# Weight conversion moved into the attention, parked in DRAM, and a re-ordered first round: one core, float32 arithmetic from float64 weights

## The chip, the cores and the metric

The kernel runs on one core of a Trainium2 chip. Its engines work side by side, each on its own list of instructions, in order: PE (TensorE, with PEld for its weight loads), DVE (VectorE), ACT (ScalarE), POOL (GpSimd) and SP (SyncE), which here only issues DMAs. The metric is the device time of one execution in microseconds. Times of parts come from the profile of one execution.

## The reference

Two layers follow each other. Linear attention with a decay per head gives x; a mixer works on x first along the tokens and then along the channels, each time with two matrices, a relu between them, and a residual.

```python
# q, k, v: (4 batches, 8 heads, 768 tokens, 64), float32; lam: one decay per head
for b in range(nb):                          # blocks of 64 tokens
    intra = einsum('bhic,bhjc->bhij', qb, kb) * Dmask       # lam ** (i - j), i >= j
    out[:, :, sl] = einsum('bhij,bhjd->bhid', intra, vb) + einsum('bhid,bhde->bhie', qb * lam_pow, kv_state)
    kv_state = lam_block * kv_state + einsum('bhsd,bhse->bhde', kb * rev_pow, vb)
x = out.transpose(0, 2, 1, 3).reshape(4, 768, 512)
h = maximum(x.transpose(0, 2, 1) @ w_tok1, 0) @ w_tok2      # 768 -> 256 -> 768
u = x + h.transpose(0, 2, 1)
result = u + maximum(u @ w_ch1, 0) @ w_ch2                  # 512 -> 1536 -> 512
```

The weights of the mixer are drawn as float64. The kernel gets them as pairs of 32-bit words and has to make float32 out of them itself.

## The kernel before, in words

**Numbers.** A matrix product in float32 is made of three fast ones: each operand x is split into a rounded high part (ACT copies it into the type float32r) and the rest (DVE or POOL subtracts the high part), and high times high, low times high and high times low are added up in PSUM. Names that end in h and l (c1h, c1l, o6h, o6l, hh, hl) are such pairs.

**Conversion.** `narrow` makes float32 from the two words of a float64 with one ACT pass (Abs of the upper word) and five DVE steps (L348 the sign bit, L351 joins the lower word's top bits to it, L354 limits, L357 shifts, L360 joins). Its steps are put into a list, `waiting`. `later(n)` takes n of them off the list and issues them (n + 1 while more than seven wait); the calls to `later` are written by hand between the parts of the main work. So the order on every engine is the order in which the program issues, and an instruction that waits holds up all that come behind it on its engine.

**Attention.** 16 iterations, each for a pair of heads of one batch (plus two ahead of the first). An iteration holds the scores of the next pair, the outputs of this one, the state, the transposes, and from the fourth on `groups` of the token mixer: `token_hidden` (18 matmuls of 256 columns) and `token_out` (6 of 384 per half), 48 groups in all, of which ten are left over for the first quad. The token weights and the first of six groups of channel weights are converted meanwhile, the latter in four pieces of 512 elements per partition (512 in float64, 1024 words).

**Channel mixer.** The activations lie in SBUF as U, transposed, in six blocks of 512 tokens. Two blocks are worked on together, with a scheme of seven products in place of eight (Strassen's kind): `product(n, s)` multiplies one of seven weight combinations (c1) with one of seven operands o1 to o7, sums and differences of U's blocks. The order of the operands is `PROD = (1, 2, 6, 7, 5, 3, 4)`. A quad n is one pair of blocks (round r = n // 6) against one of six weight groups (g = n % 6); 18 quads in three rounds. Each product is six matmuls of 512 columns into a PSUM bank (a, b or d); bank b is added to several times, and `snap` copies it to SBUF in between (L736) before PE goes on. `whole` adds a bank and a snapshot into an SBUF tile (L740), `relu` makes hh (ACT, L696) and hl of it: by DVE from the SBUF tile (L702), or in the first round, quads 0 to 4, by a second ACT pass and a POOL subtraction (L698, L699). `mm2(n, x, t)` is the second layer, six matmuls, and DVE adds its bank to U (L774). In quad n the products of n alternate with the eight `mm2` of quad n - 1.

**Weights in the first round.** Quad n converts the group of n + 1, four pieces of 512 from `raw_of`, `convert`, with `combine` for the seven sums of the first matrix: POOL forms four sums in a tile `sm` (L509 to L514), ACT and POOL split them into c1h and c1l (L493, L489), and all of this stands in the one list `waiting`. The split weights are kept in DRAM (`keep_c1`, `keep_c2`), and rounds 1 and 2 fetch them from there (`fetch_c1`, `fetch_c2`).

**Operands.** `build(r)` gives the steps that make o1 to o7 of a round: sums by DVE (L660), their split by ACT (L538) and by POOL or DVE (L539). In quad 0 the steps of an operand are issued right before its product; for later rounds they follow the product of the last quad of the round that used the same operand, all of o6's sums there.

Of the kernel before, what the change touches and what calls it, by code (L numbers as in the profile page):

```python
# [9 lines left out]
F32 = mybir.dt.float32  # L10
# [11 lines left out]
def kernel(  # L22
# [28 lines left out]
    P = 128  # L51
# [24 lines left out]
    ident = upool.tile([P, P], F32, name="ident")  # L76
    wa = ctx.enter_context(tc.tile_pool(name="wa", bufs=1))
# [258 lines left out]
    def narrow(raw, a, sg):  # L336
# [11 lines left out]
            lambda: nc.vector.tensor_scalar(  # L348
                out=sg, in0=high, scalar1=0x80000000, scalar2=None, op0=ALU.bitwise_and
            ),  # L350
# [7 lines left out]
                out=a, in0=a, scalar1=3, scalar2=0x40000000, op0=ALU.logical_shift_left, op1=ALU.bitwise_xor  # L358
            ),
            lambda: nc.vector.scalar_tensor_tensor(  # L360
                out=a, in0=a, scalar=0x7FFFFFFF, in1=sg, op0=ALU.bitwise_and, op1=ALU.bitwise_or
            ),
        ]
# [102 lines left out]
    def load_piece(g, i, raw):  # L466
        if i < 2:
            src = c1u[2 * i * P : 2 * (i + 1) * P, g * FG * 2 : (g + 1) * FG * 2]
            nc.sync.dma_start(out=raw.rearrange("p (t f) -> p t f", t=2), in_=src.rearrange("(t p) f -> p t f", p=P))
        else:  # L470
            r0 = g * FG + (i - 2) * P
            nc.sync.dma_start(out=raw, in_=c2u[r0 : r0 + P, :])

    def convert_piece(raw, a, sg):
        return narrow(raw.rearrange("p (n two) -> p n two", two=2), a, sg)
# [3 lines left out]
    def combine(n, pool, a0, a1, s, eng):  # L479

        a0, a1 = (x.bitcast(F32).rearrange("p (t w j) -> p t w j", t=2, w=2) for x in (a0, a1))
        s1, s2, s3, s4 = (s[:, w] for w in range(4))

        def low(sl, src, perm):
            hi, lo = c1s[n]
            lo, hi = lo[:, sl], hi[:, sl].bitcast(F32)
            if perm:
                lo, hi = lo.rearrange("p w t j -> p t w j"), hi.rearrange("p w t j -> p t w j")
            nc.gpsimd.tensor_sub(out=lo, in0=src, in1=hi)  # L489

        def high(sl, src, perm):
            hi = c1s[n][0][:, sl]
            nc.scalar.copy(out=hi.rearrange("p w t j -> p t w j") if perm else hi, in_=src)  # L493

        def raw0():
            c1_tiles(n, pool())
            high(0, a0[:, :, 0], False)
            low(0, a0[:, :, 0], False)
# [454 lines left out]
```

## Time and profile before

| what | us |
|---|---|
| median of three runs (lowest, highest) | 662.24 (661.59, 669.48) |
| the profiled execution | 663.17 |
| its span, first to last instruction | 661.40 |
| attention, to the first product of quad 0 | 192.49 |
| quad 0, with the last ten token groups | 47.76 |
| quads 1 to 5 | 150.30 |
| quads 6 to 17 (to the last product's end) | 249.49 |
| tail | 21.36 |

A busy time is that of an engine's own instructions, overlaps counted once; matmuls overlap, so the mean duration of one (some 0.4 us for 512 columns) is longer than the distance to the next. A row of the groups names line, engine, operation, output and inputs, the shape and the count, then total busy time and the mean of one in ns, then the idle time ahead of them on their engine and what ended it. In a wait row the first name waited for the second.

### The profile page before, as it was taken

Reading aid. Unit: us, or ns where it says so; the run is one execution under the profiler, and the core shown is the slowest. Engines: PE = TensorE matmul, PEld = TensorE weight load, DVE = VectorE, ACT = ScalarE, POOL = GpSimd, SP = SyncE. Lnnn points to the kernel's source line nnn. Section 1 sums busy time; section 2 is a strip of 40 time slices with the busy share of each in tenths; the row PEclk is TensorE's granted clock in tenths of the full one; section 3 lists DMA queues with packets and bytes.
Section 4 is the critical chain, followed back from the end, with each engine's and each line's share of the span. In section 5 each row is a group of like instructions: output and inputs, shape, how many; then the busy total and the mean of one; then the engine's idle time right before and its main releaser. Section 6 shows DMA issues by size and latency. Waiting matters only on the chain. (4 is left out here: it accounts for less than half of the span.)

```text
span 661.4 us, 9534 instructions
## 1 busy us (share of the span) xinstructions
PE 584.0 (88%) x3746; PEld 486.3 (74%) x3746; DVE 416.1 (63%) x649; ACT 201.4 (30%) x376; POOL 220.9 (33%) x198
## 2 busy tenths in 40 slices
PE   6978999799995668697976699999998999999996
PEld 5867988789984546485754578888886888888885
DVE  4578777574526549686696977444556874444554
ACT  2444323233323234234334332121214422121211
POOL 6667734666502363645536530000004300000000
PEclk9989999799998769897979889999999999999999
DMA  9996983747012107164464545644412557244105
GB/s 187 240 235 109 173 154 76 131 91 188 2 33 64 33 3 281 55 264 158 145 257 180 215 176 95 207 175 175 173 71 106 197 99 273 86 175 175 63 1 127
DMA packets 152684, 93.42 MB, mean 141 GB/s; under 512 B 136256, under 2 KB 137792, under 8 KB 152640
## 3 DMA queue, kind: packets, MB, share of 16 engines
q1 hardware_dynamic: 151440, 92.03, 48.9%
q10 hardware_dynamic: 1200, 0.79, 0.4%
q8 instruction: 29, 0.48, 0.3%
q14 instruction: 15, 0.12, 0.1%
HBM read 69.21 MB, written 23.59 MB: 140 GB/s over the span
## 5 line engine op out<-in xcount | busy, mean ns | idle before, releaser
L774 DVE TENSOR_TENSOR uT<-po,uT 128x512 f32<-128x512 f32 x144 | 98.8, 687 | 86.3 <-PE po L771 85.2
L771 PE MATMUL po<-hh,c2h 128*128 128x512 f32 x288 | 115.8, 402 | 0.0
L771 PE MATMUL po<-hl,c2h 128*128 128x512 f32 x288 | 114.9, 399 | 0.0
L771 PE MATMUL po<-hh,c2l 128*128 128x512 f32 x288 | 114.9, 399 | 0.0
L771 PEld LDWEIGHTS po<-hh,c2l 128*128 128x128 f32 x288 | 55.5, 193 | 12.9
L771 PEld LDWEIGHTS po<-hl,c2h 128*128 128x128 f32 x288 | 55.3, 192 | 13.1
L771 PEld LDWEIGHTS po<-hh,c2h 128*128 128x128 f32 x288 | 55.5, 193 | 12.7
L696 ACT ACTIVATE hh<-xu 128x512 fp32r<-128x512 f32 x36 | 22.7, 632 | 80.2 <-PE po L771 47.7
L736 ACT COPY u<-b 128x512 f32<-128x512 f32 x36 | 21.0, 584 | 83.8 <-PE b L727 83.7
L287 PE MATMUL xT<-a,vn 128*64 128x128 f32 x384 | 37.6, 288 | 6.2 <-ACT uT L304 6.1
L539 POOL TENSOR_TENSOR o1l<-uT,o1h 128x512 fp32r<-128x512 f32 x6 | 7.9, 1340 | 104.0 <-ACT o1h L538 104.0
L727 PE MATMUL b<-o6h,c1h 128*128 128x512 f32 x36 | 17.3, 482 | 25.2 <-ACT p L736 21.4
L251 POOL COPY stb<-sv 64x320 f32<-64x320 f32 x32 | 26.1, 816 | 35.4 <-DVE sv L238 34.5
L740 DVE TENSOR_TENSOR xu<-d,u 128x512 f32<-128x512 f32 x36 | 24.8, 688 | 18.3 <-ACT u L736 14.0
L212 POOL TENSOR_SCALAR kd<-kn,mask 128x320 f32<-128x320 f32 x32 | 35.9, 1132 | 0.9
L272 DVE TENSOR_TENSOR a<-sc,mask 128x384 f32<-128x384 f32 x64 | 31.2, 550 | 5.7 <-PE sc L263 5.6
L304 ACT COPY uT<-xT 128x384 f32<-128x384 f32 x32 | 15.3, 477 | 61.4 <-PE xT L297 61.4
L354 DVE TENSOR_SCALAR wa<-wa 128x512 f32<-128x512 f32 x20 | 16.4, 821 | 26.1 <-ACT wa L347 26.1
L297 PE MATMUL xT<-qs,stb 128*64 128x128 f32 x320 | 32.2, 278 | 0.0
L287 PEld LDWEIGHTS xT<-a,vn 128*64 128x64 f32 x384 | 23.3, 141 | 10.1 <-ACT uT L304 7.0
L328 DVE TENSOR_TENSOR xlo<-xp,xhi 128x384 fp32r<-128x384 f32 x32 | 17.6, 554 | 19.4 <-ACT xhi L327 19.3
L422 PE MATMUL ph<-xhi,w1h 128*128 128x256 f32 x96 | 28.3, 295 | 1.7 <-DVE uT L447 1.3
(160 smaller groups left out, 1381.5 us busy)
## 6 DMA issues: line engine op xcount, KB each, us to landing
c1h<-k1h SPq DMA_DIRECT2D x12, 896.0 KB, 4.6
c1l<-k1l SPq DMA_DIRECT2D x12, 896.0 KB, 6.5
raw<-in_moe_w_ch_dram SPq DMA_DIRECT2D x20, 512.0 KB, 4.2
kn<-in_k_dram SPq DMA_DIRECT2D x32, 192.0 KB, 3.8
vn<-in_v_dram SPq DMA_DIRECT2D x16, 384.0 KB, 5.1
c2h<-k2h SPq DMA_DIRECT2D x12, 512.0 KB, 5.5
c2l<-k2l SPq DMA_DIRECT2D x12, 512.0 KB, 6.4
k1h<-c1h SPq DMA_DIRECT2D x6, 896.0 KB, 5.7
```

What stands on the lines that cost most here:

```text
L212: nc.gpsimd.tensor_scalar_mul(kds[i][:, h], loaded[i][0][:, 0 : NC - 1, h], mask[:, 2 * p + h, P - 1 : P])
L251: nc.gpsimd.tensor_copy(out=st[r, :, h, :], in_=sv[r].rearrange("p (e c) -> p c e", c=NC - 1))
L272: nc.vector.tensor_mul(out=a, in0=sc[h].rearrange("p (c i) -> p c i", i=P), in1=mask[:, 2 * p + h, None, :].broadcast_to([P, 3, P]),)
L287: nc.tensor.matmul(out=xT[h * D : (h + 1) * D, cs], lhsT=vns[i][:, h, c, :], rhs=weights_of[i, g, h][:, cg, :], start=(cg == 0), stop=False,)
L297: nc.tensor.matmul(out=xT[h * D : (h + 1) * D, cs], lhsT=st[:, c - 1, h, :], rhs=qss[i][:, c - 1, :], start=False, stop=(cg == 2),)
L328: nc.vector.tensor_sub(out=lo, in0=src, in1=hi.bitcast(F32))
L422: nc.tensor.matmul(out=ph, lhsT=w[:, c, fs], rhs=x[:, c], start=(i == 0), stop=(i == 3 * NC - 1))
L696: nc.scalar.activation(hh, src, AF.Relu)
L736: nc.scalar.copy(out=c[nm], in_=c["b"])
L740: nc.vector.tensor_add(out=x, in0=c[bk], in1=c[nm])
L771: nc.tensor.matmul(out=po, lhsT=w[:, jj, cs], rhs=h, start=(i == 0), stop=(i == 3 * JG - 1))
L774: nc.vector.tensor_add(out=ub, in0=two(po), in1=ub)
```

## The change

- **Pieces.** A piece is now 1024 elements (both row halves of the first matrix, or both parts of the second): two pieces for a group, twelve for all. `narrow` takes the sign with an ACT pass (`Sign`, with a tiny bias held in a tile) in place of L348; `pad` puts empty turns into the list.
- **Attention.** Five pieces are converted there: both of groups 0 and 1 and the first of group 2. Group 0 is combined and split as before; the other three are written to DRAM as float32 (`park`). The scratch for it is a tile that later holds the operands o1 and o2, which become one tile. Turns of the list are now taken after hidden groups and not after output groups.
- **First round.** The other seven pieces are converted in quads 1 to 4, two a quad, and parked. `take_parked` reads a parked piece back: the first matrix of group n + 1 at the start of quad n, the second of group n in its third step. A second list, `fuse`, with its own calls `later2`, holds their combination and splitting: in `combine` the copies and the subtractions are now single steps, POOL's four sums are formed in place, and empty turns stand between the sums and their copies.
- **Relu.** `whole` adds into the PSUM bank (a, d, or a new bank e), and relu reads from there: one ACT pass, one DVE step. The slow path is gone. These steps are put off by one or more half-steps (`after`, `flush`), and `drain`, which holds the snapshots and sums, stands after the product's list turns.
- **Operands.** In quad 0 the sums and splits are issued ahead of the products (six steps before the first one, two after each product or group). For rounds 1 and 2 the sums are issued one a step in an earlier quad (the fifth of round 0, the fourth of round 1), the splits follow each product in the last quad, all on POOL.
- **Keeping.** c1h, c1l and c2 are written to DRAM later in a quad; the second tile pool for weights is opened in two parts.

```diff
-    def narrow(raw, a, sg):
+    def narrow(raw, a, sg, pad=()):
...
             lambda: nc.scalar.activation(af, high.bitcast(F32), AF.Abs),
-            lambda: nc.vector.tensor_scalar(
-                out=sg, in0=high, scalar1=0x80000000, scalar2=None, op0=ALU.bitwise_and
-            ),
+            lambda: nc.scalar.activation(sg.bitcast(F32), high.bitcast(F32), AF.Sign, bias=tiny),
+            *pad,
...
+    def park(g, i, a):
+        parked[g, i] = dr.tile([P, 4 * FG], F32, name=f"f{i}{g}")
+        nc.sync.dma_start(out=parked[g, i], in_=a.bitcast(F32))
...
+        return [
+            lambda: high(0, 1, raw0),
+            lambda: high(1, 3, u1),
+            lambda: low(0, 1, raw0),
+            lambda: low(1, 3, u1),
+            lambda: nc.gpsimd.tensor_add(out=a22, in0=a21, in1=a22),
+            lambda: nc.gpsimd.tensor_sub(out=a21, in0=a11, in1=a21),
+            lambda: nc.gpsimd.tensor_sub(out=a11, in0=a22, in1=a11),
+            lambda: nc.gpsimd.tensor_sub(out=a12, in0=a12, in1=a11),
+            *[lambda: None] * pads,
+            lambda: high(3, 5, u0),
+            lambda: high(5, 7, u1),
+            lambda: low(3, 5, u0),
+            lambda: low(5, 7, u1),
         ]
...
+    loads, turns = (4, 6, 7, 9, 10), (5, 7, 8, 10, 11)
...
+        if i in turns:
+            x = turns.index(i)
+            ng, piece = divmod(x, 2)
+            a, sg = (words(3) if x % 2 else scr)[:, 2048:3072], scr[:, 3072:]
+            waiting.extend(convert_piece(words(3)[:, :2048] if x % 2 else scr[:, :2048], a, sg))
+            waiting.append(was_read)
+            if ng > 0:
+                waiting.append(lambda ng=ng, piece=piece, a=a: park(ng, piece, a))
+            elif piece == 0:
+                waiting.extend(combine(0, lambda: wa, a))
+            else:
+                waiting.extend(split_c2(0, lambda: wa, a))
...
+        a, b = (V, G) if r == 0 else (G, G)
...
-    def relu(n, j, x, src, slow):
+    def relu(n, j, x, src):
...
-        nc.scalar.activation(hh, src, AF.Relu)
-        if slow:
-            nc.scalar.activation(src, src, AF.Relu)
-            nc.gpsimd.tensor_sub(out=hl, in0=src, in1=hh.bitcast(F32))
...
+        def whole(to, bk, nm):
+            nc.vector.tensor_add(out=c[to], in0=c[bk], in1=c[nm])
...
         elif o == 5:
             snap("u4")
-            relu(n, 1, 1, whole("d", "u4"), slow)
+            c["e"] = bank("xT", f"e{n}", CB)
+            after(lambda: whole("e", "d", "u4"), *relu(n, 1, 1, c["e"]))
...
+    def take_parked(g, i):
+        while (g, i) not in parked:
+            later(1)
+        fresh[g, i] = fp.tile([P, 4 * FG], F32, tag="fa", bufs=2, name=f"fa{g}{i}")
+        nc.sync.dma_start(out=fresh[g, i], in_=parked[g, i])
...
+    pieces = deque([(3, 0), (2, 1), (4, 0), (3, 1), (5, 0), (4, 1), (5, 1)])
...
+    sums, steps = build(0)
+    first = [*sums[:4], *steps[6], *sums[4:6], *steps[7], *steps[5], *sums[6:], *steps[4], *steps[3]]
+    for f in first[:6]:
+        f()
...
+            if 1 <= n < NG - 1 and s == 0:
+                take_parked(n + 1, 0)
+            if 1 <= n < NG - 1 and s == 2:
+                fuse.extend(combine(n + 1, lambda n=n: wa if n % 2 else w1b, fresh[n + 1, 0]))
+            if 1 <= n < NG and s == 2:
+                take_parked(n, 1)
+            if 1 <= n < NG and s == 4:
+                for f in reversed(split_c2(n, lambda n=n: w2b if n % 2 else wa, fresh[n, 1])):
+                    fuse.appendleft(f)
...
+            for q_ in range(s, s + 1 if s < 6 else 8):
+                if q_ == s:
+                    product(n, s)
+                    flush()
+                    later(1)
+                    later2(2)
+                    if sums:
+                        sums.popleft()()
+                    drain(n, s)
+                add = mm2(n - 1, 1 - q_ // 4, q_ % 4)
+                flush()
+                later(1)
+                later2(2)
+                add()
+                if n < NG and pieces:
+                    if tick % 4 == 0:
+                        convert(*pieces.popleft())
+                    if tick % 4 == 2:
+                        next_piece()
+                    tick += 1
+            if r + 1 < NR and g == NG - 1:
+                after(*nxt[o])
```

More of the change, by code (lines that the diff above doesn't have):

```diff
@@ L528 @@
     PROD = (1, 2, 6, 7, 5, 3, 4)
-    WI = {1: 0, 2: 1, 4: 2, 5: 3, 6: 4, 7: 5, 3: 6}
+    WI = {1: 0, 2: 1, 4: 2, 6: 3, 7: 4, 3: 5, 5: 6}
     NR = NB // 2
-    ops = {}
+    ops, o12 = {}, []
     def operand(r, o, pool):
+        if o < 3:
+            if not o12:
+                o12.append(oa.tile([P, 4, 2, CB], F32R, tag="o12", name="o12"))
+            ops[r, o] = [o12[0][:, 2 * (o - 1) + i] for i in range(2)]
+            return
         ops[r, o] = [pool.tile([P, 2, CB], F32R, tag=f"o{o}{t}", name=f"o{o}{t}{r}") for t in "hl"]
@@ L560, with was_read @@
     early = {4: 2, 8: 1}
-    raws = []
+    loads, turns = (4, 6, 7, 9, 10), (5, 7, 8, 10, 11)
+    read = 0
+    def was_read():
+        nonlocal read
+        read += 1
+    hidden = {groups[12 * b + f] for b in range(B) for f in range(4)}
     for i in range(-2, NI):
@@ L592 @@
                 f()
-                later(2 if len(work) < 3 else 1)
+                if i < 4:
+                    later(2 if len(work) < 3 else 1)
+                elif f in hidden:
+                    later(2)
             if n < 2 and i >= 0:
@@ L672, in build @@
         make, part = sums_of(r)
+        sums = [lambda n=n, ct=ct: make(n, ct, V) for n in (1, 2, 3, 4) for ct in range(2)]
+        a, b = (V, G) if r == 0 else (G, G)
         steps = {
@@ L731, in product, with drain @@
                 i += 1
-        slow = r == 0 and g < NG - 1
+    def drain(n, s):
+        o = PROD[s]
+        c = c_of[n]
         def snap(nm):
@@ L745, in product @@
         elif o == 2:
-            relu(n, 0, 0, whole("a", "p1"), slow)
+            whole("a", "a", "p1")
+            after(*relu(n, 0, 0, c["a"]))
         elif o == 6:
@@ L852, with next_piece @@
-    steps = build(0)
-    rest = list(groups)
-    plan = {0: 2, 1: 2, 2: 2, 3: 2, 4: 2}
+        a = wp.tile([P, 1024], U32, tag="wa", bufs=2, name=f"wa{g}{i}")
+        sg = wp.tile([P, 1024], U32, tag="ws", bufs=1, name=f"ws{g}{i}")
+        waiting.extend(convert_piece(fresh[g, i, 0], a, sg))
+        waiting.append(lambda: park(g, i, a))
+    pieces = deque([(3, 0), (2, 1), (4, 0), (3, 1), (5, 0), (4, 1), (5, 1)])
+    def next_piece():
+        if pieces:
+            raw_of(*pieces[0])
+    sums, steps = build(0)
@@ L855 @@
+    first = [*sums[:4], *steps[6], *sums[4:6], *steps[7], *steps[5], *sums[6:], *steps[4], *steps[3]]
+    for f in first[:6]:
+        f()
+    first = deque(first[6:])
+    sums = deque()
+    rest = deque(groups)
+    plan = {0: 2, 1: 4, 2: 2, 3: 2}
     NQD = NR * NG
+    tick = 0
     for n in range(NQD):
         r, g = divmod(n, NG)
-        nxt = build(r + 1) if g == NG - 1 and r + 1 < NR else None
+        if g == (NG - 2 if r == 0 else 3) and r + 1 < NR:
+            sums, nxt = build(r + 1)
+            sums = deque(sums)
```

266 lines of the change are left out of this document (116 added, 150 removed).

## The prediction

> **What bounds the kernel now.** I first cut the span into stages at the first product matmul of a quad (a quad is one pair of 512-token blocks against one group of the channel weights; there are 18, in three rounds of six). The stage table gives the busy time of PE, PEld, DVE, ACT and POOL, the granted clock, the share and the rate of the DMA engines; its stages are the attention, quad 0, quads 1 to 5, quads 6 to 17, and the tail. Below it stand the first matmuls of quads 0, 1, 6, 11 and 12 (start, duration).
>
> ```profile
> span 661.4 us, 9534 instructions
> ...
> 0.00:192.49 192.49, 171.70 (x2026) 156.12 (x2027) 123.89 (x227) 66.94 (x145) 112.92 (x112) 0.97 0.68 136
> 192.49:240.25 47.76, 29.95 (x128) 23.69 (x127) 25.14 (x36) 13.72 (x25) 15.84 (x13) 0.78 0.14 45
> 240.25:390.55 150.30, 119.82 (x452) 93.19 (x451) 114.73 (x162) 58.95 (x102) 77.33 (x62) 0.88 0.46 175
> 390.55:640.04 249.49, 246.68 (x1070) 200.62 (x1069) 141.46 (x209) 58.97 (x99) 14.80 (x11) 1.00 0.45 147
> 640.04:661.40 21.36, 15.83 (x76) 12.68 (x75) 10.93 (x16) 2.88 (x5) 0.00 (x0) 0.96 0.46 98
> ```
> ```profile
> 192.49 0.39 PE L727 MATMUL b<-o1h,c1h 128*128 128x512 f32 x1
> ...
> 240.25 0.63 PE L727 MATMUL b<-o1h,c1h 128*128 128x512 f32 x1
> ...
> 390.55 0.39 PE L727 MATMUL b<-o1h,c1h 128*128 128x512 f32 x1
> ...
> 494.30 0.40 PE L727 MATMUL b<-o1h,c1h 128*128 128x512 f32 x1
> ...
> 518.12 0.39 PE L727 MATMUL b<-o1h,c1h 128*128 128x512 f32 x1
> ```
>
> Quads 6 to 10 take (494.30 - 390.55) / 5 = 20.75 us each, with a full clock and PE without a gap: 15 sets of six matmuls (7 products, 8 of the second layer), 1.383 us a set. That is the floor of a quad. Quad 11 takes 23.82, so 3.1 us go where the operands of round 2 are built. Quads 1 to 5 take 150.30 where the floor is 103.75: 46.5 us lost, at a clock of 0.88. Quad 0 takes 47.76 with PE busy for 29.95 of it. The lost time is thus in the first round, where the weights are still being converted. The waits there name the cause; they are the rows "who waited for whom" with total, times and longest, and one PE row with the wait ahead of it.
>
> ```profile
> ACT c1h L493 <- POOL sm L514: 24.1, 5, 5.6
> ...
> PE b L727 <- ACT p L736: 21.4, 4, 5.6
> ```
> ```profile
> 381.00 0.79 PE L727 MATMUL b<-o3h,c1h 128*128 128x512 f32 x1 [5.93 <-ACT u L736]
> ```
>
> ACT takes its instructions in order. Its copy of the four weight sums waits for POOL, 24.1 us in five times, and behind it stands the snapshot of bank b, without which PE may not go on adding to b: four times 5.4 us. At 381 the same bank waits for a snapshot that stands behind the operands of round 1, which DVE, ACT and POOL build one after the other.
>
> **Quad 0.** The operand sums (eight DVE subtractions) were made just ahead of the product that needs them; now four, and the two halves of operand 6, are issued ahead of the quad, the rest two at a time beside the first products and token groups. PE's own work is 7 sets, 9.7 us; two hidden groups of 18 matmuls at (198.07 - 195.07) / 25 = 0.120, 4.3 us; eight output groups of 6 at (201.48 - 199.57) / 11 = 0.174, 8.3 us: 22.3 in all.
>
> ```profile
> 195.07 0.28 PE L422 MATMUL ph<-xhi,w1l 128*128 128x256 f32 x1
> ...
> 198.07 0.28 PE L422 MATMUL ph<-xlo,w1h 128*128 128x256 f32 x1
> ...
> 199.57 0.34 PE L442 MATMUL pu<-w2h,hh 128*128 128x384 f32 x1
> ...
> 201.48 0.34 PE L442 MATMUL pu<-w2l,hh 128*128 128x384 f32 x1
> ```
> ```profile
> L774 DVE TENSOR_TENSOR uT<-po,uT 128x512 f32<-128x512 f32 x144 | 98.8, 687 | 86.3 <-PE po L771 85.2
> ...
> L740 DVE TENSOR_TENSOR xu<-d,u 128x512 f32<-128x512 f32 x36 | 24.8, 688 | 18.3 <-ACT u L736 14.0 <-PE d L727 3.5
> L351 DVE SCALAR_TENSOR_TENSOR ws<-raw,ws 128x512 uint32<-128x512 uint32 x20 | 20.7, 1034 | 0.5
> L702 DVE SCALAR_TENSOR_TENSOR hl<-xu,hh 128x512 fp32r<-128x512 f32 x26 | 17.8, 686 | 4.7 <-ACT hh L696 4.5
> L447 DVE TENSOR_TENSOR uT<-pu,uT 128x384 f32<-128x384 f32 x32 | 17.7, 553 | 15.7 <-PE pu L442 15.7
> ...
> L354 DVE TENSOR_SCALAR wa<-wa 128x512 f32<-128x512 f32 x20 | 16.4, 821 | 26.1 <-ACT wa L347 26.1
> L357 DVE TENSOR_SCALAR wa<-wa 128x512 uint32<-128x512 uint32 x20 | 14.4, 720 | 0.5
> ...
> L360 DVE SCALAR_TENSOR_TENSOR wa<-wa,ws 128x512 uint32<-128x512 uint32 x20 | 13.8, 691 | 0.6
> ...
> L660 DVE TENSOR_TENSOR tt<-uT 128x512 f32<-128x512 f32 x12 | 10.2, 890 | 0.0
> ...
> L348 DVE TENSOR_SCALAR ws<-raw 128x512 uint32<-128x512 uint32 x20 | 10.2, 509 | 0.2
> ...
> L354 DVE TENSOR_SCALAR uT<-uT 128x512 f32<-128x512 f32 x9 | 3.7, 413 | 0.0
> ...
> L539 DVE TENSOR_TENSOR o4l<-tt,o4h 128x512 fp32r<-128x512 f32 x3 | 4.3, 1420 | 2.1 <-ACT o4h L538 2.1
> ```
>
> DVE has 8 x 0.89 of sums, 4 low halves at up to 1.42, 8 additions at 0.55 and six steps of about 0.69: 21.3 us, nearly as much as PE, but a part of it starts before the quad. No conversion is left in quad 0. The third product on bank b still follows its snapshot with nothing between; I take 24 us, with 22.3 (PE alone) and 32 (a third of DVE's work in line with PE) as ends: -23.8 (-25.5 to -15.8).
>
> **Quads 1 to 5.** The wait of ACT for the weight sums goes: between the issue of the lows and the copy of the sums now lie four POOL additions, three empty turns and, from quad 1 on, the four steps that split the second weights. At four turns in each step of 2.77 us (two sets) that is some 8 us for POOL work that has to be done. The slow relus (two ACT passes and a POOL subtraction, 15 times) become one ACT pass and one DVE step from PSUM, 15 x 0.686 = 10.3 us more for DVE, about 2 a quad. The parts of round 1's operands leave DVE for POOL and follow product by product, their sums made a quad earlier: the wait at 381 goes, and quad 11's 3.1. What is late next are two things.
>
> First DVE. A quad needs 8 additions, 3 sums of banks and 4 lows, 15 x 0.687 = 10.3 us. A converted piece of 1024 has four DVE steps (the sign moves to ACT). Twice the means of L351, L354, L357 and L360 make c = 2 x (1.034 + 0.821 + 0.720 + 0.691) = 6.53 us. Two pieces in each of quads 1 to 3 make 23.4 us against 20.75; quad 4 has five quarters of a piece and seven sums, 10.3 + 8.2 + 6.2 = 24.7. The four are 3 x 2.6 + 3.9 = 11.7 us over; quad 5 is light, and three PSUM banks let DVE lag some 4 us: 8 us of it reach PE.
>
> These means hold waits on POOL. A DVE step that comes behind a started POOL subtraction ends late:
>
> ```profile
> 255.62 1.28 POOL L370 TENSOR_TENSOR c2l<-wa,c2h 128x512 fp32r<-128x512 f32 x1 [1.74 <-ACT c2h L369]
> ```
> ```profile
> 255.87 1.58 DVE L351 SCALAR_TENSOR_TENSOR ws<-raw,ws 128x512 uint32<-128x512 uint32 x1
> ```
>
> DVE's step took 1.58 where the same kind at L360 has 0.691, and POOL's ends at 256.90, 0.55 before it. The Trainium skill (SBUF — State Buffer, "SBUF: two separate sides") says why: DVE and GpSimd share a port pair, whoever starts first has it for its whole instruction and the other is blocked. By that rule the wait belongs to the instruction and not to the element, so a step of twice the size would wait once: L351 loses 0.34 (against L360), L354 and L357 0.41 and 0.31 (against the undisturbed 0.413), and c would be 5.5, the excess of the four quads some 4 us, none of it reaching PE. I keep 6.53; the row of POOL says that the longer steps hold POOL up as well.
>
> Second, a new wait. Each piece is written to DRAM and read back by a DMA that must wait for the write. SP, which issues both, stands at that wait, with the loads and the keeping of weights behind it (none of them is needed within the quad). In quads 2 to 4 the second weights' piece ends its conversion about 2 us into the quad that splits it; write and read take from 2 x 4.2 to 2 x 8.1 us by the rows for 512 KB:
>
> ```profile
> raw<-in_moe_w_ch_dram SPq DMA_DIRECT2D x20, 512.0 KB, 4.2
> ...
> k2l<-c2l SPq DMA_DIRECT2D x6, 512.0 KB, 8.1
> ```
> ```profile
> L347 ACT ACTIVATE wa<-raw 128x512 f32<-128x512 f32 x20 | 13.0, 663 | 0.6 <-DMA raw<-in_moe_w_ch_dram 0.6
> ...
> L538 ACT CAST o6h<-tt 128x512 fp32r<-128x512 f32 x6 | 3.6, 619 | 10.5 <-DVE tt L660 10.5
> ...
> L193 ACT ACT_TABLE_LOAD x1 | 1.3, 1283 | 1.2 <-PEq L939 1.2
> ```
>
> ACT's two copies of that piece stand ahead of the snapshot that the product on bank b awaits after five steps, 13.8 us. Two copies and the snapshot at 0.62 make 1.9: ready at 2 + 8.4 + 1.9 = 12.3, no loss, or at 2 + 16.2 + 1.9 = 20.1, 6.3 lost. I take 3 in each of three quads, 9, between the two rows. While PE waits there DVE catches up, so the 8 and the 9 do not add: 10 us over the floor, ends 0 and 25. Quads 1 to 5: -36.5 (-46.5 to -21.5). Traffic is no bound: ten pieces out and in are 10 MB more at a DMA share of 0.46, in three quarters of the time. Keeping the weights later in a quad costs nothing, as they are read a round later.
>
> **The attention.** It converts five pieces of 1024 where it had four of 512. DVE: 5 x 6.53 - 4 x (3.27 + 0.51), and six sign steps less at 0.51: +14.5 us on 123.89 of 192.49. ACT: ten passes at 2 x 0.663 and six at 0.663 in place of four: +14.6 on 66.94. Both engines stay under three quarters, but an ACT pass twice as long stands before the copies that PE waits for. Ends: 0 and 15 (all of DVE's); I take 5, nearer to the busy shares. The first operand's copy waits for the parking of group 2's piece out of the same buffer; an iteration (192 / 16 = 12 us) lies between, above the 8.1 of the row, and without it ACT would stand for those 8 us.
>
> **Sum.** The profiled execution took 663.17 us, 1.8 more than its span and 0.9 above the median of 662.24. 663.2 + 5 - 23.8 - 36.5 - 3.1 = 604.8, and 604 as a median.
>
> **Rivals.** *All is hidden:* no cost in the attention, quad 0 at PE's 22.3, no excess: 663.2 - 25.5 - 46.5 - 3.1 = 588, 587 as a median. For it: POOL's part gets easier. Against: 23.4 us of DVE in 20.75.
>
> *DVE becomes the bound:* the whole 14.5 in the attention, 11.7 and 9 in the quads without overlap: 663.2 + 14.5 - 23.8 - 46.5 + 20.7 - 3.1 = 625. For it: DVE is in order and PE needs it at every set. Against: 77% (114.73 / 150.30) was its highest share so far.
>
> *Sign needs another table:* Abs, Copy and Relu alternate now with the one load in the row. If each of 18 Sign passes (11 in the attention, 7 in the round) brought two loads of 1.283, the round would bear 18 us and the attention perhaps half of 28: 604 + 32 = 636. The Trainium skill (ScalarE: Activation LUTs, "Table sets: the hidden batching unit") names relu, copy, identity and abs as part of every set, not sign; by its 2.66 us a switch the same shares would give 670, an estimate; no run here shows a Sign.
>
> *Slower: DVE and POOL block each other on the long steps.* At a cost c per piece the excess is 3 x (2c - 10.45) + (1.25c - 4.25) + (5c - 18.2), even with all of the attention's on the path. The gains of 73.4 without excess are eaten up when that passes 73.4, at c = 10.4, 1.6 times what the means give; at c = 11 it is 671. For it: the row of 1.58. Against: in that row DVE waited for the rest of one POOL step and no more, and the means have such rows in them.
>
> **Chances.** Forecast 0.62 (own range 595 to 614), all hidden 0.13, DVE bound 0.16, tables 0.04, slower 0.05. The range from 591 to 630 leaves out the better half of the second case, the worst of the third and the last two, some 2 in 10. About 2%, 13 us, can be told from no change: under 649 lie the first three and most of the fourth, 0.92; the rest of it and the milder end of the last give 0.04 for no change and 0.04 for slower.
>
> **What would show it.** Right: in the profile after, the wait of ACT for the weight sums and of PE for the first snapshot are gone; quad 0 takes 22 to 28 us, quads 1 to 5 some 114, quads 6 to 17 249 less 3, at a clock of 1.0. PE waits left in quads 2 to 4 sit ahead of the product with operand 3, behind a split of second weights that waits for a DMA. Wrong: DVE steps of 1024 over 2 us on average and DVE above 95% in quads 1 to 3 (DVE bound), more than one table load, or an attention that ends after 207.

## The result, and the profile after

| what | before, us | forecast, us | after, us |
|---|---|---|---|
| median (lowest, highest) | 662.67 (661.59, 669.48) | 604 | 606.85 (605.61, 608.10), four runs each |
| the profiled execution, and its span | 663.17, 661.40 | 604.8, - | 605.85, 604.10 |
| attention, to the first product of quad 0 | 192.49 | +5 | 196.63 (+4.1) |
| quad 0 | 47.76 | 24 | 27.39 (-20.4) |
| quads 1 to 5 | 150.30 | 113.8 | 113.41 (-36.9) |
| quads 6 to 17 | 249.49 | -3.1 | 245.31 (-4.2) |
| tail | 21.36 | 21.36 | 21.36 |

The ratio of the times is 0.9138, with a 95% interval of 0.9072 to 0.9204: faster, inside the range and 2.9 us above the forecast. The rows of the table come from the stage table of the changed kernel: start and end, length, busy time of PE, PEld, DVE, ACT and POOL, granted clock, DMA share and GB/s. In order: attention, quad 0, quads 1 to 5, quads 6 to 17, tail.

```profile
0.00:196.63 196.63, 172.43 (x2026) 155.36 (x2027) 128.53 (x221) 78.94 (x158) 116.06 (x114) 0.98 0.71 148
196.63:224.02 27.39, 24.43 (x129) 21.66 (x127) 17.89 (x27) 10.71 (x21) 13.03 (x12) 0.94 0.30 86
224.02:337.43 113.41, 105.93 (x451) 85.20 (x450) 87.86 (x114) 55.48 (x91) 72.42 (x55) 0.98 0.79 287
337.43:582.74 245.31, 245.31 (x1070) 200.71 (x1069) 135.69 (x202) 57.55 (x99) 22.43 (x18) 1.00 0.47 154
582.74:604.10 21.36, 15.78 (x76) 12.65 (x75) 10.91 (x16) 2.85 (x5) 0.00 (x0) 0.96 0.48 98
```

Quads 1 to 5 are 37 us shorter, while the DMA share rose from 0.46 to 0.79. From one first product to the next, the five take 20.40, 21.82, 23.36, 27.42 and 20.41 us; in the kernel before they took 26.10, 29.79, 28.02, 28.38 and 38.01. So 17.6 of the 36.9 us come from quad 5 alone, where the kernel before held PE twice, for 5.54 and 5.93 us, at a granted clock of 0.82.

The waits of the first round (from quad 0 to the end of quad 5; the first name waited for the second: total, times, longest):

```profile
ACT hh L742 <- DVE a L778: 14.8, 5, 5.9
...
ACT c2h L529 <- DMA fa<-f: 11.0, 4, 3.8
...
PE b L762 <- ACT u L775: 8.2, 6, 2.3
ACT wa L350 <- DMA raw<-in_moe_w_ch_dram: 7.6, 3, 3.1
...
PE pu L446 <- DVE uT L451: 2.3, 1, 2.3
```

ACT's wait for POOL's weight sums, 24.1 us before, is gone. PE waits 8.2 us for bank b in place of 21.4 for the first snapshot and 5.9 for the one at 381. New are two waits of ACT for DMAs: for parked pieces (11.0) and for raw weights (7.6).

The conversion's steps (line, engine, operation, shape, count, total, mean in ns, wait ahead) are these; the last row is the only table load of the whole run:

```profile
L362 DVE SCALAR_TENSOR_TENSOR wa<-wa,ws 128x1024 uint32<-128x1024 uint32 x7 | 9.9, 1408 | 0.1
L353 DVE SCALAR_TENSOR_TENSOR ws<-raw,ws 128x1024 uint32<-128x1024 uint32 x7 | 9.7, 1379 | 3.5 <-ACT ws L351 3.5
L356 DVE TENSOR_SCALAR wa<-wa 128x1024 f32<-128x1024 f32 x7 | 9.1, 1298 | 0.0
...
L351 ACT ACTIVATE ws<-raw,tiny 128x1024 f32<-128x1024 f32 x7 | 8.5, 1216 | 0.0
L350 ACT ACTIVATE wa<-raw 128x1024 f32<-128x1024 f32 x7 | 7.9, 1131 | 7.6 <-DMA raw<-in_moe_w_ch_dram 7.6
L359 DVE TENSOR_SCALAR wa<-wa 128x1024 uint32<-128x1024 uint32 x7 | 6.2, 884 | 0.0
...
L196 ACT ACT_TABLE_LOAD x1 | 1.3, 1283 | 1.2 <-PEq L1017 1.2
```

A piece costs DVE 1.408 + 1.379 + 1.298 + 0.884 = 4.97 us. Eighteen Sign passes brought no second table.

What a late quad looks like is seen in quad 3 (it starts at 266.24), on DVE, then ACT, then PE:

```profile
271.61 1.21 DVE L362 SCALAR_TENSOR_TENSOR wa<-wa,ws 128x1024 uint32<-128x1024 uint32 x1
272.74 0.68 DVE L822 TENSOR_TENSOR uT<-po,uT 128x512 f32<-128x512 f32 x1
273.34 0.69 DVE L778 TENSOR_TENSOR a<-a,p 128x512 f32<-128x512 f32 x1
```

```profile
274.06 0.60 ACT L742 ACTIVATE hh<-a 128x512 fp32r<-128x512 f32 x1 [4.69 <-DVE a L778]
274.56 1.13 ACT L350 ACTIVATE wa<-raw 128x1024 f32<-128x1024 f32 x1
275.58 1.21 ACT L351 ACTIVATE ws<-raw,tiny 128x1024 f32<-128x1024 f32 x1
276.67 0.93 ACT L501 CAST c1h<-fa 128x256 fp32r<-128x256 f32 x2
277.49 0.60 ACT L775 COPY u<-b 128x512 f32<-128x512 f32 x1
```

```profile
278.14 0.50 PE L762 MATMUL b<-o5h,c1h 128*128 128x512 f32 x1 [0.83 <-ACT u L775]
```

DVE does the last step of a piece, then an addition of the second layer, and only then the sum of bank a; it has worked without a gap since 265.78. ACT's relu waits 4.69 us for that sum; behind the relu stand Abs, Sign and two copies of the weight sums, and behind those the snapshot of bank b for which PE waits. The waiting row names ACT's snapshot; its lateness began on DVE. Whether that is the cause, or the two waits for DMAs are, was the question for the runs.

### The profile page after: what moved, and what is told of

It reads as the page before. It is cut to its first block, busy times and chain, and to the rows that moved or that the text cites. A ratio compares the mean times of both kernels' runs of the same rounds, so it can differ in the third digit from the quotient of the medians.

```text
span 604.1 us, 9525 instructions
## 1 busy us (share of the span) xinstructions
PE 563.9 (93%) x3746; PEld 475.6 (79%) x3746; DVE 380.9 (63%) x578; ACT 205.5 (34%) x373; POOL 223.9 (37%) x198
## 4 chain that ended last, share of the span: by engine, by line
PE 60%; DVE 8%; DMA 5%; ACT 4%; issue 1%; ACTq 0%; DVEq 0%; SPq 0%
PE po L813 28%; PE b L762 14%; PE d L762 7%; PE a L762 3%; PE pu L446 3%; DMA fa<-f 2%; DMA raw<-in_moe_w_ch_dram 1%; DMA f<-wa 1%; PE ph L426 1%; PE xT L290 1%; DVE ws L353 1%; DVE tt L698 1%; PE sc L266 1%; PE xT L300 1%; DVE uT L822 1%
## 5 line engine op out<-in xcount | busy, mean ns | idle before, releaser
L813 PE MATMUL po<-hh,c2l 128*128 128x512 f32 x288 | 113.4, 394 | 0.0
L813 PE MATMUL po<-hh,c2h 128*128 128x512 f32 x288 | 113.3, 394 | 0.0
L813 PE MATMUL po<-hl,c2h 128*128 128x512 f32 x288 | 113.1, 393 | 0.0
L562 POOL TENSOR_TENSOR o<-uT,o 128x512 fp32r<-128x512 f32 x12 | 15.4, 1293 | 109.4 <-ACT o L561 108.1
L504 POOL TENSOR_TENSOR c1l<-fa,c1h 128x512 fp32r<-128x512 f32 (+1 forms) x20 | 30.1, 1523 | 39.3 <-ACT c1h L501 39.3
L254 POOL COPY stb<-sv 64x320 f32<-64x320 f32 x32 | 27.5, 860 | 43.4 <-DVE sv L241 42.5
L742 ACT ACTIVATE hh<-d 128x512 fp32r<-128x512 f32 x18 | 10.8, 600 | 58.1 <-PE po L813 48.0
L446 PE MATMUL pu<-w2h,hh 128*128 128x384 f32 x64 | 23.4, 366 | 4.4 <-DVE uT L451 3.2
L266 PE MATMUL sc<-qT,kT 64*128 64x128 f32 x384 | 27.1, 290 | 0.2 <-ACT qT L209 0.2
```

The source lines that it names most:

```text
L254: nc.gpsimd.tensor_copy(out=st[r, :, h, :], in_=sv[r].rearrange("p (e c) -> p c e", c=NC - 1))
L266: nc.tensor.matmul(out=sc[h][:, c * P : (c + 1) * P], lhsT=kTs[i][r, cs], rhs=qTs[i][r, cs], start=True, stop=True,)
L446: nc.tensor.matmul(out=pu, lhsT=h[:, kk, cs], rhs=w[:, kk, ss], start=(i == 0), stop=(i == 3 * NK - 1))
L504: nc.gpsimd.tensor_sub(out=of(1, w0, w1), in0=src, in1=of(0, w0, w1).bitcast(F32))
L813: nc.tensor.matmul(out=po, lhsT=w[:, jj, cs], rhs=h, start=(i == 0), stop=(i == 3 * JG - 1))
```

## The experiments

**Two theories on quads 1 to 5.** Mine, on record: the gain comes from ACT's order (no wait for POOL ahead of a snapshot), and what is left is part DVE's excess, part the new wait for the piece that is written and read back. The rivals: the gain has another source (pieces, relu from PSUM), and what is left is only the one or only the other. The runs that were compared with the kernel before in several rounds have a ratio; the others are one execution, beside one of 665.12 us of the kernel before. The times of quads come from one execution each: in the profiles of four kernels that have quads 1 to 5 alike, single quads differ by up to 1.5 us and the five together by 0.9 (112.58 to 113.48).

### The gain in quads 1 to 5: ACT's order

No empty turns between POOL's sums and their copies, and the split of the second weights behind them:

```diff
-    def combine(n, pool, a, pads=3):
+    def combine(n, pool, a, pads=0):
...
-                for f in reversed(split_c2(n, lambda n=n: w2b if n % 2 else wa, fresh[n, 1])):
-                    fuse.appendleft(f)
+                fuse.extend(split_c2(n, lambda n=n: w2b if n % 2 else wa, fresh[n, 1]))
```

> The changed kernel, with the copies of the weight sums issued right behind POOL's four sums (no empty turns, and the split of the second weights behind them instead of between). Theory (ACT's order: a copy that waits for POOL holds up the snapshot that PE needs): POOL needs some 6 us from the first subtraction to the third sum, the copies come after some 4, so ACT waits 2 us or more for POOL in each of quads 1 to 4, PE waits for a snapshot behind that, quads 1 to 5 grow from 113 to 119 to 126 us, the time to 612 to 620. Rival (it was the amount of work on DVE and POOL, not the order of ACT's copies): ACT's wait may appear, but quads 1 to 5 stay within 2 us of 113 and the time at 605 to 609.

It took 616.71 us; quads 1 to 5 took 21.34, 27.49, 26.76, 27.61 and 20.43, together 123.6. In the waits of its quads 1 to 5 the old one is back:

```profile
ACT c1h L501 <- POOL fa L513: 22.3, 4, 5.9
```

The empty turns and the place of the split are worth 10 us, all of it in quads 1 to 4. Nothing of the arithmetic differs, so the order in which ACT and POOL get these steps is a cause by itself. It accounts for 10.2 of the 19.3 us that quads 1 to 4 gained. Quad 5 stays at 20.43, so its 17.6 us have another source. The earlier sums of round 1's operands and the conversion that has left the quad are the likely ones, but no run takes them apart.

### Quad 0: the order alone

First the operand steps of quad 0 right ahead of their products, in the changed kernel:

```diff
-    first = [*sums[:4], *steps[6], *sums[4:6], *steps[7], *steps[5], *sums[6:], *steps[4], *steps[3]]
-    for f in first[:6]:
-        f()
-    first = deque(first[6:])
+    own = {6: [*sums[:4], *steps[6]], 7: [*sums[4:6], *steps[7]], 5: steps[5], 3: steps[3], 4: [*sums[6:], *steps[4]]}
+    first = deque()
...
             if n == 0:
+                for f in own.get(o, []):
+                    f()
```

> The changed kernel, with the operand steps of quad 0 issued right ahead of the product that needs them, as before the change. Theory (quad 0's 20 us came from the order of these steps): quad 0 goes from 27.4 back to 42 to 48 us, the time to 621 to 628. Rival (quad 0 became shorter because the conversion of group 1 left DVE, ACT and POOL, and the order matters little): quad 0 stays below 33, the time at 606 to 612.

618.33 us, and quad 0 took 40.33, a little under what I had expected: the early order is worth 13 of the 20.4 us here. Then the opposite, the early order of quad 0 in the kernel before, with the two halves of operand 6 issued and shared between DVE and POOL as the change has them:

```diff
-                lambda: part(6, 2, 0, G),
                 lambda: make(2, 1, V),
-                lambda: part(6, 2, 1, V),
+                lambda: part(6, 2, 0, V),
+                lambda: part(6, 2, 1, G),
...
+    first = [*steps[6], *steps[7], *steps[5], *steps[4], *steps[3]]
+    for f in first[:6]:
+        f()
+    first = deque(first[6:])
...
-                for f in steps.pop(o, []) if o > 2 else []:
-                    f()
...
             product(n, s)
+            for _ in range(2 if first else 0):
+                first.popleft()()
```

> The kernel before, with one thing changed: the operand steps of quad 0 are issued early (six ahead of the quad, two after each product or group), as the change does. Theory (quad 0's order is worth its 20 us only once the conversion of group 1 has left that quad, because the two fill DVE and POOL together): quads 0 and 1, 73.9 us together, fall by 6 to 14 us, the time is 648 to 656. Rival (the order alone gives it all): they fall by 18 us or more, the time is 645 or less.

643.34 us. Quad 0 fell from 47.76 to 25.38; quad 1, which took 26.1 in the kernel before, took 30.04. Together 55.4 in place of 73.9: 18.4 us for an order of steps, with the conversion still in the quad. My expectation that the conversion had to leave the quad first was wrong; its steps fit beside PE once no operand is made at the last moment.

### The price of DVE's steps

Each step of 1024 is done as two of 512, all else equal:

```diff
+        m = a.shape[1] // 2 if pad else a.shape[1]
+        sl = [slice(i, i + m) for i in range(0, a.shape[1], m)]
...
+            for c in sl:
+                nc.vector.tensor_scalar(
+                    out=af[:, c], in0=af[:, c], scalar1=HIGH_MIN, scalar2=HIGH_MAX, op0=ALU.max, op1=ALU.min
+                )
```

> The changed kernel, with each of the four DVE steps of a 1024 piece issued as two steps of 512, back to back. Theory (DVE's wait for POOL belongs to the instruction, so more and shorter steps wait more often): the DVE time of a piece in the first round goes from 4.97 to 6.3 to 6.8 us (fixed costs add some 0.6, the waits of 1.2 double), quad 4 grows, the time is 608 to 613. Rival (the wait grows with the elements): the piece goes to about 5.5 us by the fixed costs alone, the time is 606 to 608.

```profile
L354 DVE SCALAR_TENSOR_TENSOR ws<-raw,ws 128x512 uint32<-128x512 uint32 x14 | 15.0, 1115 | 3.5 <-ACT ws L378 3.5
L372 DVE SCALAR_TENSOR_TENSOR wa<-wa,ws 128x512 uint32<-128x512 uint32 x14 | 14.4, 1066 | 0.0
L360 DVE TENSOR_SCALAR wa<-wa 128x512 f32<-128x512 f32 x14 | 11.8, 880 | 0.0
L366 DVE TENSOR_SCALAR wa<-wa 128x512 uint32<-128x512 uint32 x14 | 7.9, 605 | 0.0
```

A piece costs 2 x (1.115 + 1.066 + 0.880 + 0.605) = 7.33 us in place of 4.97; quads 1 to 5 take 123.3, the whole 616.4. So twice the elements in one step is far from twice the time. Some 0.6 of the 2.36 us between the two are the cost of four more steps without any wait, an estimate from the shortest step of either size on each of the four lines in the changed kernel (3.72 us a piece in steps of 1024, 2 x 2.16 in steps of 512). The rest agrees in direction with the Trainium skill's rule (SBUF — State Buffer, "SBUF: two separate sides": where DVE and GpSimd need the port pair that they share, the second is blocked until the first one's instruction ends); its size went beyond what I had set for it, and why is open. My doubling of the means of 512, 6.53, was the wrong price for a step of 1024.

### What is left in quads 1 to 5: the round trip or DVE

The split of the second weights one step later, with more empty turns in `combine`, should have taken ACT's wait for the parked piece off the path:

```diff
-            if 1 <= n < NG and s == 4:
+            if 1 <= n < NG and s == 5:
                 for f in reversed(split_c2(n, lambda n=n: w2b if n % 2 else wa, fresh[n, 1])):
...
-                fuse.extend(combine(n + 1, lambda n=n: wa if n % 2 else w1b, fresh[n + 1, 0]))
+                fuse.extend(combine(n + 1, lambda n=n: wa if n % 2 else w1b, fresh[n + 1, 0], 7))
```

> The changed kernel, with the split of the second weights issued one step later (in the sixth step of a quad, behind the snapshot and not ahead of it). Theory (PE's waits ahead of operand 3's product in quads 2 to 4, 0.7 and 1.5 and 2.3 us, are ACT standing at the DMA that reads the parked piece): these waits go, quads 1 to 5 fall from 113.4 to between 108 and 110.5, the time by 3 to 5 us to 602 to 604. Rival (DVE is what is late in these quads, and the DMA only comes with it): quads 1 to 5 stay within 1 us of 113.4, the time at 605 to 607.

Ratio 0.9168 (0.9113 to 0.9222), median 608.65, which can't be told apart from the changed kernel; in the profiled execution, the longest of four (605.94 to 612.10), quads 1 to 5 took 118.5 in place of 113.4. The wait of PE ahead of the product with o3 went, and others came, as the waits of PE in quads 1 to 5 show:

```profile
PE b L762 <- ACT u L775: 5.7, 2, 3.4
PE po L813 <- DVE uT L822: 2.8, 3, 1.5
PE d L762 <- DVE e L778: 1.2, 1, 1.2
```

That was a first sign against the round trip. Next, DVE's side: round 1's sums, seven of which fall into quad 4, moved to quad 5, two a step.

```diff
-        if g == (NG - 2 if r == 0 else 3) and r + 1 < NR:
+        if g == (NG - 1 if r == 0 else 3) and r + 1 < NR:
```

> The changed kernel, with the eight operand sums of round 1 made in quad 5, two a step, and no longer in quad 4, one a step. Theory (quad 4's 27.4 us are DVE's: 25.8 us busy): without 6 to 7 us of sums quad 4 falls to between 22 and 24.5, quad 5 stays below 21.5, the time falls by 2.5 to 5 us to 602 to 604. Rival (quad 4 waits for the DMA of the parked piece, whatever DVE does): quad 4 stays above 26, the time at 605 to 607.

Ratio 0.9047 (0.8971 to 0.9124), executions between 596.97 and 606.46; the whole can't be told apart from the changed kernel's 0.9138 (0.9072 to 0.9204). The quads say more: quad 4 fell from 27.42 to 24.81 (26.23 at the least in the profiles of the four kernels), and quads 1 to 5 took 110.3 where those four have 112.6 or more. DVE's share in quad 4 is real. Then the round trip itself was taken away, the split reading the converted tile in SBUF:

```diff
-        waiting.append(lambda: park(g, i, a))
+        if i == 0:
+            waiting.append(lambda: park(g, i, a))
+        else:
+            waiting.append(lambda: direct.__setitem__(g, a))
...
-                take_parked(n, 1)
+                (take_parked(n, 1) if n == 1 else take_direct(n))
```

> The changed kernel, but the pieces of the second weights of groups 2 to 5 are no longer written to DRAM and read back: their split reads the converted tile in SBUF, at the same place in the quad. Theory (the prediction's new wait: SP stands at the write and the read behind it, ACT at the copy of a piece that has not come back, and the raw loads behind both come late): the waits of ACT at c2h for a DMA go from 11.0 us to under 4 (the one of quad 1 stays), the waits of SP at a read of a parked piece fall by half, quads 1 to 5 take 105 to 110 where they took 113.4, the whole 598 to 603. Rival (the loss of these quads is DVE's, which is only seen through the wait that ends last): quads 1 to 5 stay at 111 to 115, the whole 604 to 608, and ACT waits at the copy for DVE, or at Abs for POOL, which now frees the converted tile.

Median 606.33, ratio 0.9133 (0.9108 to 0.9158): no gain. Quads 1 to 5 took 20.40, 21.80, 23.54, 27.97 and 20.43, together 114.1. The waits of its quads 1 to 5:

```profile
ACT wa L350 <- POOL c2l L532: 5.9, 2, 3.0
...
ACT wa L350 <- DMA raw<-in_moe_w_ch_dram: 4.0, 2, 2.2
...
ACT c2h L529 <- DMA fa<-f: 0.9, 1, 0.9
```

ACT's wait for the parked piece fell from 11.0 to 0.9 and the quads stayed as long. A new wait, 5.9 us of Abs for the tile that POOL now frees, clouds the reading. The last run therefore left the round trip as it is and took DVE's steps of the seven pieces away (groups 2 to 5 then hold other weights):

```diff
-        waiting.extend(convert_piece(fresh[g, i, 0], a, sg))
+        cv = convert_piece(fresh[g, i, 0], a, sg)
+        waiting.extend(cv[:2] + [lambda: None] * (len(cv) - 2))
```

> The changed kernel without DVE's four steps for the seven pieces that are converted in quads 1 to 4 (their loads, both ACT passes, the writes and reads of the parked pieces, the splits and the combining stay; groups 2 to 5 then hold other weights, so the output is not the reference's). Some 7 x 4.97 = 35 us of DVE go, and with them POOL's waits for the port. Theory (after the run with the direct split: the 11.4 us that quads 1 to 5 stand above five quads of 20.4 are DVE's, seen through whatever wait ends last): quads 1 to 5 take 102 to 104.5, the whole 594 to 598. Rival (they are the loads that come late, a DMA share of 0.9 and the order of ACT): quads 1 to 5 take 108 to 113, the whole 601 to 606, and ACT's waits at Abs and at c2h for a DMA stay near 7.6 and 11.0 us. In between, DVE's part is what goes.

Median 596.89, ratio 0.8984 (0.8936 to 0.9032). Its stage row of quads 1 to 5, its waits there, and its ACT in quad 3 (which starts at 267.51):

```profile
226.23:329.24 103.01, 103.01 (x451) 84.50 (x450) 57.87 (x86) 55.80 (x91) 59.79 (x55) 1.00 0.88 315
```

```profile
ACT c2h L529 <- DMA fa<-f: 8.7, 4, 2.8
...
ACT wa L350 <- DMA raw<-in_moe_w_ch_dram: 2.0, 1, 2.0
```

```profile
272.60 0.60 ACT L742 ACTIVATE hh<-a 128x512 fp32r<-128x512 f32 x1 [2.92 <-DVE a L778]
273.10 1.13 ACT L350 ACTIVATE wa<-raw 128x1024 f32<-128x1024 f32 x1
274.12 1.20 ACT L351 ACTIVATE ws<-raw,tiny 128x1024 f32<-128x1024 f32 x1
275.23 0.92 ACT L501 CAST c1h<-fa 128x256 fp32r<-128x256 f32 x2
276.04 0.58 ACT L775 COPY u<-b 128x512 f32<-128x512 f32 x1
```

PE is busy for all of the 103.01 us, at a clock of 1.00. ACT still waits 8.7 us for parked pieces, in four quads as before, and PE waits for nothing. The same five instructions of ACT stand in the same order; the relu starts 272.60 - 267.51 = 5.1 us into the quad, where the changed kernel has 274.06 - 266.24 = 7.8. So the 113.41 - 103.01 = 10.4 us that the changed kernel loses in these quads come with DVE's steps, and neither the round trip nor a DMA share of 0.88 costs anything by itself. The late raw loads lose much of their wait too (7.6 to 2.0); that it follows DVE and does not lead it is an inference from this run, not measured alone. POOL's busy time falls as well, from 72.42 to 59.79 us for the same 55 instructions, so the run takes away with DVE's steps what they cost POOL; in the changed kernel no wait of PE, DVE or ACT in these quads ends with POOL.

### The attention

DVE's four steps left out for the three parked pieces of groups 1 and 2:

```diff
-            waiting.extend(convert_piece(words(3)[:, :2048] if x % 2 else scr[:, :2048], a, sg))
+            cv = convert_piece(words(3)[:, :2048] if x % 2 else scr[:, :2048], a, sg)
+            waiting.extend(cv if ng == 0 else cv[:2] + [lambda: None] * (len(cv) - 2))
```

> The changed kernel without DVE's four steps for the three pieces of groups 1 and 2 that are converted and parked in the attention (their loads, both ACT passes and the writes stay; groups 1 and 2 then hold other weights, so the output is not the reference's). Some 12 DVE steps of about 1.2 us, 15 us of DVE, go. Theory (the attention's 4.1 us more are DVE's longer and more numerous steps, between which PE's and ACT's other work waits): the attention ends at 192 to 194 and the whole takes 601 to 604. Rival (they are ACT's passes of twice the length, or the loads): it ends at 196 to 199 as before, the whole at 605 to 608.

The attention ended at 194.0, the whole took 603.10 (ratio 0.9082, 0.9047 to 0.9117). In the profiles of nine kernels with the attention unchanged it ended between 196.1 and 199.75. That is 2.1 us below the lowest of the nine, in one execution against a spread of 3.7; the median is 3.2 below the 606.33 of the kernel with the direct split, measured beside it. So some 2 or 3 of the 4.1 us are likely to be DVE's steps in these pieces; the rest stays open.

### Two smaller questions and a combination

Quads 6 to 17 now alternate: 20.88 us for even n, 20.43 for odd n (before: 20.77 and 20.72). I shifted the weight and operand tiles to places that are multiples of 128 bytes.

```diff
-    tiny = upool.tile([P, 1], F32, name="tiny")
+    tiny = upool.tile([P, 32], F32, name="tiny")[:, 0:1]
...
+    edge.tile([P, 24], F32, name="edge")
```

> The changed kernel, with the tile of the tiny bias made 128 bytes a partition instead of 4, and 96 bytes set aside at the other end of SBUF, so that all weights and operands start at multiples of 128 bytes. Theory (quads 7, 9, 11 take 20.43 us and quads 6, 8, 10 take 20.88 by where their weights and operands lie): all quads of rounds 1 and 2 take 20.4 to 20.5, the time falls by 2 to 3.5 us to 603 to 605. Rival (the place in SBUF is not what makes the difference): the pattern of 20.43 and 20.88 stays, the time at 605 to 607.

Ratio 0.9114 (0.9059 to 0.9169), median 605.09: even quads 20.76, odd ones 20.43. Of the 0.45 us between them 0.12 goes with the place; the rest is open.

The later split, the later sums and the shift together, and one hidden group of the token mixer moved from the attention's last iteration to quad 0:

```diff
-    take = {4: 2, 5: 2, 6: 5, 7: 4, 8: 2, 9: 4, 10: 5, 11: 2, 12: 2, 13: 5, 14: 4, 15: 1}
+    take = {4: 2, 5: 2, 6: 5, 7: 4, 8: 2, 9: 4, 10: 5, 11: 2, 12: 2, 13: 5, 14: 4}
...
-    plan = {0: 2, 1: 4, 2: 2, 3: 2}
+    plan = {0: 3, 1: 4, 2: 2, 3: 2}
```

> The two shifts and the alignment together, and the last hidden group of the attention moved to quad 0, so that DVE's sums of round 0 are not queued behind it. Theory (DVE's lag and the read of the parked pieces are the two causes of the 10 us over the floor in quads 1 to 5, and DVE's late start costs quad 0 its 2.3 us wait): quads 1 to 5 take 104 to 107, quad 0 with the moved group no more than 28, the time is 594 to 599. Rival (something else comes late in their place, DVE's conversions above all): quads 1 to 5 stay above 109, the time at 600 to 604.

Median 605.95, ratio 0.9123 (0.9075 to 0.9171): quads 1 to 5 took 116.7, the late split losing what the sums gain. Without the late split and the shift, with the direct split in their place:

> The changed kernel with three edits: the split straight from SBUF, round 1's operand sums in quad 5, and one hidden group more in quad 0 and one less in the attention's last iteration. If both losses are separate (DVE's in quad 4, worth 3.1 us in quads 1 to 5 alone, and the round trip's), quads 1 to 5 take 102 to 107 and the whole 594 to 600. If they are one loss seen in two places, quads 1 to 5 take 108 to 111 and the whole stays at 601 to 605.

Median 599.86, ratio 0.9037 (0.9004 to 0.9069), 6.5 us below the kernel with the direct split alone, in the same comparison. The stage rows:

```profile
0.00:193.26 193.26, 169.73 (x2008) 152.78 (x2009) 127.25 (x219) 78.39 (x157) 115.99 (x114) 0.98 0.73 151
193.26:220.15 26.89, 25.08 (x148) 22.66 (x146) 18.57 (x29) 11.28 (x23) 13.04 (x12) 1.00 0.29 88
220.15:329.41 109.26, 105.23 (x452) 83.75 (x450) 91.36 (x114) 55.26 (x91) 70.10 (x53) 1.00 0.74 259
```

Quads 1 to 5 take 109.3, 1.0 less than with the later sums alone: one loss seen in two places, as the rival had it. The time that I had set for the theory came out all the same, through the attention and quad 0 (220.15 in place of 224.02). From the later sums alone (0.9047) its ratio can't be told apart.

## Why the prediction was right

**The time.** The four stages changed by +4.1, -20.4, -36.9 and -4.2, where +5, -23.8, -36.5 and -3.1 were forecast. The largest term came out within half a microsecond, and that was luck in part: it is a gain less a loss, and the terms of the loss were wrong and cancelled.

**Quads 1 to 5, the gain: right as far as it is shown.** ACT's wait for POOL's sums held the snapshots; the run without empty turns brings it back, with 10.2 of the 19.3 us of quads 1 to 4. That the 17.6 us of quad 5 come from the operands of round 1 fits the wait at 381, which is gone, but was not tested alone.

**Quads 1 to 5, the loss: the size right by luck, four steps wrong.** "Twice the means of L351, L354, L357 and L360 make c = ... 6.53 us" was 4.97. Where "quad 4 has five quarters of a piece", it has two pieces: of the seven first steps of DVE two stand in quad 1, one in quad 2, two in quad 3, and two in quad 4, which starts at 289.60:

```profile
290.04 1.22 DVE L353 SCALAR_TENSOR_TENSOR ws<-raw,ws 128x1024 uint32<-128x1024 uint32 x1
...
301.68 1.23 DVE L353 SCALAR_TENSOR_TENSOR ws<-raw,ws 128x1024 uint32<-128x1024 uint32 x1 [1.43 <-ACT ws L351]
```

With c = 4.97 the prediction's own sum gives quads 1 to 3 at most 2 x 4.97 + 10.3 = 20.2 us, under PE's 20.4, and quad 4 10.3 + 2 x 4.97 + 6.2 = 26.4. The stage rows of quads 2, 3 and 4 (busy time of PE, PEld, DVE, ACT and POOL, as above):

```profile
244.42:266.24 21.82, 21.14 (x91) 16.83 (x90) 17.24 (x23) 10.16 (x16) 10.56 (x9) 1.00 0.90 314
266.24:289.60 23.36, 21.03 (x92) 16.74 (x90) 18.04 (x24) 10.79 (x18) 13.40 (x10) 1.00 0.82 299
289.60:317.02 27.42, 22.96 (x91) 17.86 (x90) 25.80 (x33) 10.77 (x19) 18.13 (x12) 0.94 0.67 248
```

Without DVE's steps these three quads took 20.88, 20.43 and 20.87 us, so they lose 0.94, 2.93 and 6.55. DVE's excess, the prediction's first reason, thus exists, but in quad 4 alone: 25.80 us of work against 20.87. The lag of "some 4 us" that "three PSUM banks" were to allow did not hide it: the quad loses more than the excess of 4.9, and with the sums in quad 5 it still lost 3.9, with DVE busy for 20.82 us. In quads 2 and 3 DVE is busy for 79% and 77%, and a budget for each quad, as I had made it, finds none of their 3.9 us. The rows of quad 3 point at the order: a conversion step of 1.21 us ahead of the sum that ACT's relu awaits, with Abs, Sign and the copies behind that relu and the snapshot last. That the order costs these 3.9 us apart from the load is argued from those rows; no run moves the steps and keeps them all. "Second, a new wait" was given 9 us: the wait exists, 11.0 us of ACT's, and has no cost that shows (8.7 us of it stand beside a PE that never waits). A price too high, too few pieces in quad 4, a lag that was not there and a wait that costs nothing cancel in "10 us over the floor".

**The sign that misled.** I had named "PE waits left in quads 2 to 4 ... ahead of the product with operand 3, behind a split of second weights that waits for a DMA" as the mark of the new wait. Such waits are there:

```profile
282.67 0.50 PE L762 MATMUL b<-o3h,c1h 128*128 128x512 f32 x1 [1.51 <-ACT u L775]
```

In quads 3 and 4 they follow a PE that had already been held ahead of the product with o5 (in quad 3 at 278.14); in quad 2 the wait of 0.69 us stands alone. With DVE's steps gone all of them vanish while ACT's wait for the DMA stays. The mark was met and did not prove the cause.

**Of what SP holds back, "none of them is needed within the quad": wrong in part.** Behind SP's waits stand the raw loads, and ACT's Abs waited 7.6 us for them. I had no price for a load of 1 MB; the rows of the DMAs (size, median time from issue to landing) have it:

```profile
raw<-in_moe_w_ch_dram SPq DMA_DIRECT2D x7, 1024.0 KB, 6.8
...
fa<-f SPq DMA_DIRECT2D x10, 512.0 KB, 5.3
...
f<-wa SPq DMA_DIRECT2D x7, 512.0 KB, 4.1
```

Traffic was no bound, as said: 315 GB/s at a share of 0.88 stood beside a PE without a gap.

**Quad 0: 24 forecast, 27.39 measured.** The mechanism was right and is shown from both sides (13 us in the changed kernel, 18.4 over two quads in the one before). Mis-sized was the part of DVE's work that "starts before the quad":

```profile
197.25 0.42 DVE L431 SCALAR_TENSOR_TENSOR hl<-ph,hh 128x256 fp32r<-128x256 f32 x1 [1.49 <-ACT hh L430]
197.59 1.28 DVE L698 TENSOR_TENSOR tt<-uT 128x512 f32<-128x512 f32 x2
```

```profile
209.31 0.44 PE L446 MATMUL pu<-w2h,hh 128*128 128x384 f32 x1 [2.29 <-DVE uT L451]
```

The sums were issued ahead of the quad but stand behind the low half of the attention's last hidden group, so DVE begins them 1 us into the quad, and PE waits 2.29 us for an addition. Behind this wait the granted clock is 0.73 (to 210.84) and then 0.59 (to 214), and six matmuls with o6 start 0.43 us apart in place of 0.23; so PE was busy for 24.43 us where 22.3 had been reckoned. In the last combination, where the hidden group stands in the quad and no longer ahead of the sums, the wait is 1.1 us, the clock 1.00, and the quad takes 26.89 with 2.2 us more of PE's work in it.

**Quads 6 to 17.** The 3.1 of quad 11 went (20.43 now, 23.82 before); the other 1.1 are the balance of odd quads at 20.43 and even ones at 20.88, which I had not foreseen.

**The attention.** 4.1 us for 5; some 2 or 3 of them are likely to be DVE's steps.

**The rivals.** "All is hidden" failed at quad 0, in the attention and in the 10.4 us. "DVE becomes the bound" had the right engine, and in quad 4 the right mechanism; over the five quads DVE was at 77%, and its 20.7 us of loss without overlap were 10.4. Sign brought no table load. POOL and DVE did not block each other to the point of being slower: the steps take 0.88 to 1.41 us.

## What to carry to other kernels

A share of busy time over several stages hides the one that is full: DVE's 77% over five quads was 94% in the quad that lost most. Count by quad which steps the list really puts there. Where an engine is not full and others still wait for it, look at what stands ahead of the instruction that they await, and follow one late matmul back through two or three engines. A wait in the table that is new and long may still cost nothing: take away the work that is suspected and see whether the bound engine's gaps go, before building on the wait's name. Issuing the steps of a start-up phase early can be worth as much as taking work out of it.

## What the runs showed of the hardware that was not expected

Matmul streams without a gap do not all run at one pace: the 90 matmuls of a quad take 20.88 us in even quads and 20.43 in odd ones, at a granted clock of 1.00, and 20.77 and 20.72 in the kernel before. The placement of the weight and operand tiles by 128 bytes moved the even ones to 20.76 and not the odd ones.

A DVE step of 1024 took less than two of 512 by a third (4.97 against 7.33 us a piece) beside the same work on POOL.
